# A mixer kernel with TensorE split in two lanes: twelve narrow products instead of four ahead of the next chunk's u, and two seeds at other places

## Chip, cores and metric

One core of a Trainium2 chip. The metric is the device time of one execution in microseconds (us); the median of three runs is given, and one further execution was profiled.

## What is computed

The first step is a short causal convolution with weights that depend on the position (softmax over 7 taps, 8 heads of 24 channels); the second is a mixer over tokens and then over channels. Cut to what matters:

```python
w = softmax(weight_gen)                       # 8 x 4096 x 8 heads x 7 taps
x = sum over k of w[..., k] * x_pad[s + k]    # 8 x 4096 x 192
h = relu(x.T @ w_tok1) @ w_tok2               # over the 4096 tokens, 256 wide
u = x + h.T
out = u + relu(u @ w_ch1) @ w_ch2             # over the channels, 192 -> 1536 -> 192
```

All matrix products are made in more than one pass with operands split into a high part and a low part (`u_hi`, `u_lo`, `w_hi`, `w_lo`), since one pass is not exact enough.

## The kernel before, in words

The 8 x 4096 rows are cut into 64 chunks of 512 rows, `g` = 0 to 63, eight to a sequence. For each chunk TensorE (PE) does four things: six pairs of channel-1 products `ph(p)` (p = 0 to 5, 192 to 1536 channels, written to PSUM tiles `w`), the channel-2 products (into two PSUM banks `acc`: `acc[0]`, the wide part of the sum with three passes, and `acc[1]`, the narrow part with two), the second token product of the next chunk (tile `up`, from which `u` of chunk g + 1 is made), and one first token product (tile `th`) for a chunk of the next sequence. ScalarE (ACT) and VectorE (DVE) turn each `ph(p)` into `h` (`take`: ACT line 799 then DVE line 800 for p < 4; two halves each of lines 792 and 793 for p = 4 and 5), make the taps of the convolution (DVE lines 278 and 292), the parts of u, and the stores (ACT line 897).

The order of all instructions is written out beforehand by a planner in the kernel. It keeps a clock for each engine (`at`, `lane_at`), adds a fixed cost for each operation (`SLOT` 226.7 ns for a 512-column product, `HOP` 60 ns from one engine to another) and issues in the order of these clocks. The engines then run their lists in order, held up by semaphores alone. The planner's costs set the order, not the time on the chip.

In chunks 16 to 54 (`in_lanes`) PE is used as two halves: every product over 128 rows is made as two products over 64 rows, one on the upper half and one on the lower, which run side by side. Each half is a lane with a list of its own (`lanes`); `run_lanes` always issues the product that can start earliest, so PE has one queue in which products of the two lanes alternate. Both lanes add into the same PSUM banks, but never in the same stretch: a bank belongs to the lane that came first (`owner`), and after that lane's last product a no-op on DVE or ACT, whichever the planner has freer (`relay`, line 1389), waits for it; the other lane's first product waits for the no-op (`behind`).

After the six `ph(p)` comes the `section` (line 1467). In it each lane has four lists: `a` and `la`, 36 products each into `acc[0]`; `c` and `lc`, 24 each into `acc[1]`; `u` and `lu`, 10 each into `up`; and 16 each into `th`. The upper lane goes a, u, c, th; the lower lane part of lc, lu, the rest of lc, th, la. So each bank is handed over once. Before the first product into `up` ACT must have copied `xb` into it (line 664, the seed of `up`); before the first product into `th` ACT must have copied the sum so far into it (line 609, `seed_one`). The seed of `up` is issued in `begin`, right behind `take(4)`; the seed of `th` is issued by a hook in the list of a lane (`seed_late`), or, where no hook stands, when the lane reaches the product (`open_one`).

The tiles `w` (for `ph`, `up` and `th`) rotate over three PSUM tiles; `ph(3)` reuses the tile of `ph(0)` and waits for its `take`. The store of a chunk begins when the lower lane has finished `la` (`finish`). One chunk in lanes, the first, has two token products (`early` and `late`), since the lead of the token products is one short there: the kernel makes 40 token products in 39 chunks.

Of the kernel before, what the change touches and what calls it, by code (L numbers as in the profile page):

```python
# [22 lines left out]
def mixer_kernel(ctx: ExitStack, tc: tile.TileContext, x, wg, wt1, wt2, wc1, wc2, out):  # L23
# [798 lines left out]
    def lanes_channel2(g, p):  # L822

        h = [ht[g, p][:, j] if (g, p) in ht else spare[(p - HB) * 2 + j] for j in range(2)]
        parts = []
        for n, steps in ((0, ((A_HI, 0), (A_LO, 0), (A_HI, 1))), (1, ((C_HL, 0), (C_HL, 1)))):
            parts.append([[(SLOT, ("acc", n, g), product(acc_t[g][n], w2s[rows, 2 * p + j, d], h[j][rows, l, :],
                                                      stop=p == NP - 1 and j == 1 and i == len(steps) - 1))
                           for j in range(2) for i, (d, l) in enumerate(steps)] for rows in HALVES])
        return parts  # L830
# [90 lines left out]
    HOP = 60  # L921
# [26 lines left out]
    def on(engine, cost, *after):  # L948
        at[engine] = max(at[engine], *after, 0.0) + cost
        return at[engine] + HOP  # L950

    class Chain:
# [4 lines left out]
        def next(self):  # L957
            self.item = next(self.items, None)
# [23 lines left out]
    def add_chain(items, wait=None, key=None):  # L982

        chains.append(Chain(items, max(at["pe"], at["dve"]) + LOAD if wait is None else wait, key))
# [39 lines left out]
    def need(what, *keys):  # L1024
        while not what():
            state["late"] = True
            at["pe"] += 500
            pump(at["pe"] + SLACK, keys)
        state["late"] = False
# [10 lines left out]
    AHEAD = 2  # L1040
    MOVES = 2
    LANE_TIGHT = 600
    HANDOVER = 60
    state = {"token1": NCH - 1, "token2": -1, "vals": 0, "few": 0, "few_t": 0, "late": False, "jobs": deque(),
             "summed": NCH - 1, "turned": FT - 1, "parts": NCH - 1, "kept": FT - 1, "stored": -1, "out": -1,
             "done": NCH - 1, "w1": NCH + 1, "channel1": 0, "rest": 0, "open": 0}
# [209 lines left out]
    late = ctx.enter_context(tc.tile_pool(name="late", bufs=1))  # L1256
# [65 lines left out]
    def token1_ready(soon=100):  # L1322
        return ready and ready[0][0] in w1t and max(ready[0][1], w1_at.get(ready[0][0], 0.0)) <= at["pe"] + soon
# [21 lines left out]
    lanes, lane_at = [deque(), deque()], [0.0, 0.0]  # L1345
    owner, turn, count = {}, {}, {}
# [3 lines left out]
    def behind(ins, of):  # L1350

        tc.add_manual_dep(ins.ins, of.ins.name, SYNC, reason="a bank goes to the other half of the rows")
# [3 lines left out]
    def lane_start(s):  # L1356

        while lanes[s] and lanes[s][0][0] == 0:
            at["pe"] = max(at["pe"], lane_at[s]) if s == 0 else at["pe"]
            lanes[s].popleft()[2]()  # L1360
        if not lanes[s]:
            return None
        bank, t = lanes[s][0][1], lane_at[s]
        if bank in owner and owner[bank] != s:
            if bank not in turn:
                return None
            t = max(t, turn[bank][1] + HANDOVER)
        return t

    def run_lanes(until):  # L1370

        while True:
            starts = [lane_start(s) for s in range(2)]
            if until():
                return
            s = min((t, s) for s, t in enumerate(starts) if t is not None)[1]
            cost, bank, fn = lanes[s].popleft()
            ins = fn()
            lane_at[s] = starts[s] + cost
            if bank is not None:  # L1380
                if owner.setdefault(bank, s) != s:
                    if bank in turn:
                        behind(ins, turn.pop(bank)[0])
                        owner[bank] = s
                else:
                    count[bank] = count.get(bank, 0) + 1
                    if count[bank] == ITEMS[bank[:2]]:
                        by, eng = min((("dve", nc.vector), ("act", nc.scalar)), key=lambda x: at[x[0]])
                        relay = eng.nop(nofuse=True)  # L1389
                        behind(relay, ins)  # L1390
                        turn[bank] = relay, on(by, 60, lane_at[s] + HOP)
            if s == 0:
                at["pe"] = lane_at[0]

    def hook(fn):

        return 0, None, fn

    def chunk_in_lanes(g):
# [32 lines left out]
        def new_one(first):  # L1432
            m, t = ready.popleft()
            lists, state["open"] = [[], []], m
            owner.update({("th", r, m): first for r in range(KR)})
            return {"m": m, "ready": max(t, w1_at.get(m, 0.0)), "lists": lists, "it": token1(m, lists, first)}

        def seed_one(one):
            next(one["it"])
            t = w_at.popleft()  # L1440
            one["at"] = on("act", 900, one["ready"], t, h1s_at[0]) if one["m"] % NCH else max(one["ready"], t)
# [19 lines left out]
        def spread(items, every=3):  # L1461
            for n, item in enumerate(items):
                if n % every == 0:
                    yield hook(quiet)
                yield item

        def section():
            next(box["two"])
            parts = [lanes_channel2(g, p) for p in range(NP)]
            (a, la), (c, lc) = ([[x for part in parts for x in part[n][s]] for s in range(2)] for n in range(2))  # L1470
            u, lu = ([hook(lambda s=s: not_before(s, box["two_at"])), *box["t2"][s]] for s in range(2))
            late = [hook(lambda s=s: open_one("late", s)) for s in range(2)]
            if "early" in box:
                early = [hook(lambda s=s: open_one("early", s)) for s in range(2)]
                upper = [early[0]] + a + u + [hook(end_two)] + c + [late[0]]
                lower = lc[:8] + [early[1], hook(lambda: end_one("early"))] + lu + lc[8:] + la \
                    + [hook(finish), late[1], hook(lambda: end_one("late"))]
            elif box["late"]:
                upper = a + u + [hook(end_two), *c, late[0], hook(lambda: end_one("late"))]
                lower = lc[:4] + lu + lc[4:14] + [hook(lambda: seed_late(1))] + lc[14:] + [late[1]] + la  # L1480
            else:
                upper = a + u + [hook(end_two)] + c
                lower = lc[:4] + lu + lc[4:] + la
            if not twice:
                lower.append(hook(finish))
            box["end"] = lane_at[0] + sum(x[0] for x in upper) + (twice or box["late"]) * T1
            top.extend(spread(upper))
            top.append(hook(lambda: box.update(done=True)))
            low.extend(lower)

        def seed_late(s):
            need(lambda: token1_ready(20 * SLOT), ("w1", state["token1"] + 1), ("x", state["token1"] + 1))
            one = box["late"] = new_one(s)
            seed_one(one)

        def open_one(key, s):
            if box[key] is True:
                seed_late(s)
            one = box[key]
            if not one["lists"][s]:  # L1500
                next(one["it"])
            not_before(s, one["at"])
            lanes[s].extendleft(reversed(one["lists"][s]))

        def end_one(key):
            t = max(lane_at) + HOP
            pump(t + SLACK_M, (), t + SLACK_A)
            m, it = box[key]["m"], box[key]["it"]
            state["token1"] = m
            free["xh"] = t  # L1510
            next(it, None)
            h1s_at[0] = on("act", 900, t)
            w_at.append(h1s_at[0])
            if m % NCH == NCH - 1:
                h1_at[m // NCH] = on("dve", 1200, on("act", 420, on("dve", 550, w_at[-1])))
            while state["w1"] < min(m + 2, NG - 1):
                state["w1"] += 1
                add_chain(load_w1(state["w1"]), key=("w1", state["w1"]))
# [24 lines left out]
        if not low:  # L1543
            between(at["pe"])
        top.append(hook(lambda: before(0)))
        run_lanes(lambda: "done" in box)

    def not_before(s, t):

        lane_at[s] = max(lane_at[s], t)  # L1550
# [11 lines left out]
    for g in range(NG):  # L1562
# [7 lines left out]
        if lanes[1]:  # L1570
            run_lanes(lambda: not lanes[1])
            at["pe"] = max(at["pe"], lane_at[1])
            need(lambda: g in ut)
# [111 lines left out]
```

## Time and profile before

| | |
|---|---|
| median of three runs | 2068.48 us (2068.37 to 2068.87) |
| the profiled execution's own time | 2068.67 us |
| its span, first to last instruction | 2066.9 us |
| around the span | 1.8 us |
| PE busy with products | 2033.7 us, 98% of the span |
| DVE busy | 1501.7 us, 73% |
| ACT busy | 1449.3 us, 70% |
[...]

Busy time of PE is the time in which at least one product runs. Where two lanes run side by side, a lane that stands still while the other runs does not show in it, and since the ends of products are modelled and overlap, neither does a short gap. What a lane loses is read from the starts of its products in the order of time, and from the list of waits of PE's weight loads (PEld), one of which stands ahead of each product.

### The profile page before, as it was taken

How to read it: one execution, taken by the hardware profiler on the slowest of the kernel's cores; microseconds unless marked ns; L12 is line 12 of the kernel's file. 1: busy time of each engine (PE TensorE's matmuls, PEld its weight loads, DVE VectorE, ACT ScalarE, POOL GpSimd, SP SyncE). 2: the span in 40 equal slices, each digit the busy share in tenths (PEclk: the TensorE clock that was granted, in tenths of full speed). 3: DMA queues.
4: the chain of work that ended last, by engine and by line, in shares of the span. 5: the costliest groups of instructions: out<-in, count | busy, mean ns of one | idle time of the engine just before them, and what ended most of it. 6: DMA issues, size and time to landing. Idle time of an engine off the chain costs nothing.

```text
span 2066.9 us, 39312 instructions
## 1 busy us (share of the span) xinstructions
PE 2033.7 (98%) x16201; PEld 1737.9 (84%) x16201; DVE 1501.7 (73%) x1813; ACT 1449.3 (70%) x2360; POOL 210.6 (10%) x292
## 2 busy tenths in 40 slices
PE   7999999999999999999999999999999999999999
PEld 7878888888888888888888888888888889888887
DVE  9899888888987768777778777768778774343343
ACT  7887667677766676776766677667677667676665
POOL 1101111111111101101101110101100110000000
PEclk9999999999999999999999999999999999999999
DMA  9878778787886766766767666666666663222121
GB/s 337 276 228 230 198 210 230 210 237 199 231 220 174 194 173 167 192 180 171 191 160 197 182 169 185 176 174 190 179 172 181 173 160 117 72 68 62 51 64 24
DMA packets 180928, 361.93 MB, mean 175 GB/s; under 512 B 26138, under 2 KB 129178, under 8 KB 165004
## 3 DMA queue, kind: packets, MB, share of 16 engines
q1 hardware_dynamic: 145420, 225.35, 35.4%
q0 software_dynamic: 35328, 134.07, 27.8%
q8 instruction: 127, 2.08, 0.4%
q14 instruction: 53, 0.43, 0.1%
HBM read 222.77 MB, written 70.52 MB: 142 GB/s over the span
## 4 chain that ended last, share of the span: by engine, by line
PE 79%; DVE 14%; ACT 5%; issue 2%; ACTq 0%; DMA 0%; DVEq 0%
PE acc L469 22%; PE w L469 21%; PE acc L811 15%; PE ph L782 10%; DVE h L800 5%; PE w L782 5%; DVE pr L278 2%; PE up L676 2%; ACT h L799 2%; ACT w L664 2%; PE th L648 2%; DVE pr L292 1%; DVE prk L404 1%; DVE h_spare L793 1%; PE w L676 1%
## 5 line engine op out<-in xcount | busy, mean ns | idle before, releaser
L469 PE MATMUL acc<-h,w2s 64*128 64x512 f32 x3120 | 556.5, 388 | 0.0
L469 PEld LDWEIGHTS acc<-h,w2s 64*128 64x128 f32 x3120 | 441.3, 184 | 34.6
L469 PE MATMUL w<-u_hi,w_hi 64*128 64x512 f32 x1404 | 370.9, 389 | 0.0
L469 PE MATMUL w<-u_hi,w_lo 64*128 64x512 f32 x1404 | 368.7, 387 | 0.0
L469 PE MATMUL w<-u_lo,w_hi 64*128 64x512 f32 x1404 | 368.4, 386 | 0.0
L469 PE MATMUL acc<-h_spare,w2s 64*128 64x512 f32 x1560 | 335.6, 386 | 0.0
L811 PE MATMUL acc<-h,w2s 128*128 128x512 f32 x1400 | 325.6, 390 | 0.0
L799 ACT ACTIVATE h<-w 128x1024 fp32r<-128x1024 f32 x210 | 215.6, 1027 | 148.7 <-PE w L469 80.8
L278 DVE TENSOR_TENSOR pr<-xc,wg 128x768 f32<-128x768 f32 x336 | 313.0, 945 | 0.2
L811 PEld LDWEIGHTS acc<-h,w2s 128*128 128x128 f32 x1400 | 261.8, 188 | 54.4 <-issue 0.7
L800 DVE SCALAR_TENSOR_TENSOR h<-w,h 128x1024 fp32r<-128x1024 f32 x210 | 255.7, 1218 | 71.0 <-ACT h L799 70.5
L296 POOL DMA_DIRECT2D xa<-pr x168 | 146.7, 873 | 1374.2 <-DVE pr L292 1002.2
L469 PEld LDWEIGHTS acc<-h_spare,w2s 64*128 64x128 f32 x1560 | 258.4, 184 | 23.4
L469 PEld LDWEIGHTS w<-u_hi,w_hi 64*128 64x128 f32 x1404 | 250.8, 184 | 24.1 <-DVE h L800 2.9
L469 PEld LDWEIGHTS w<-u_hi,w_lo 64*128 64x128 f32 x1404 | 253.8, 184 | 20.0
L469 PEld LDWEIGHTS w<-u_lo,w_hi 64*128 64x128 f32 x1404 | 254.9, 184 | 17.0
L688 DVE TENSOR_TENSOR uf<-w,uf 64x512 f32<-64x512 f32 x47 | 32.1, 683 | 256.5 <-ACT uf L684 256.5
L897 ACT COPY out_tile<-oa 32x256 f32<-32x256 f32 x504 | 203.7, 404 | 7.6
L469 PE MATMUL w<-w,h 64*128 64x512 f32 x780 | 194.9, 393 | 11.0 <-ACT w L664 11.0
L469 PEld LDWEIGHTS w<-xh,w 64*128 64x128 f32 x1280 | 187.6, 186 | 6.6 <-ACTq L1389 0.8
L469 PE MATMUL w<-xh,w 64*128 64x384 f32 (+1 forms) x1280 | 192.2, 300 | 0.6 <-ACTq L1389 0.4
L469 PEld LDWEIGHTS w<-w,h 64*128 64x128 f32 x780 | 140.7, 184 | 40.3 <-ACT w L664 26.9
(147 smaller groups left out, 3192.3 us busy)
## 6 DMA issues: line engine op xcount, KB each, us to landing
w<-s SPq DMA_DIRECT2D x96, 1024.0 KB, 6.5
xa<-pr POOLq DMA_DIRECT2D x168, 384.0 KB, 4.9
xc<-in_x_dram POOLq DMA_DIRECT2D x42, 960.0 KB, 9.6
out_dram<-out_tile SPq DMA_DIRECT2D x128, 192.0 KB, 2.6
xb<-xs SPq DMA_DIRECT2D x348, 64.0 KB, 5.1
xs<-t SPq DMA_DIRECT2D x56, 384.0 KB, 3.3
raw<-in_moe_w_tok_dram SPq DMA_DIRECT2D x16, 1024.0 KB, 8.3
xc<-in_x_dram POOLq DMA_DIRECT2D x12, 840.0 KB, 10.5
```

Of the source, the lines that this page charges most:

```text
L278: nc.vector.tensor_mul(t.rearrange("p t (h g) -> p (t h) g", h=H).rearrange("p (o n) g -> p o n g", o=1), x_k, w)
L296: nc.gpsimd.dma_start(xat[m].rearrange("p t d -> p (t d)"), tap_sums[m].rearrange("p t d -> p (t d)"), accum_op=ALU.add)
L469: return lambda: nc.tensor.matmul(to, w, v, start=start, stop=stop, skip_group_check=True)
L648: nc.tensor.matmul(to, w[:, c, r * P:(r + 1) * P], xat[m][:, c, :], start=c == first, stop=c == last, skip_group_check=True)
L664: nc.scalar.copy(up.rearrange("p k (n b c) -> p (k n) c b", c=W, b=Q), xb.rearrange("p k (n c b) -> p (k n) c b", c=W, b=Q))
L676: nc.tensor.matmul(up[:, n, :], h1[:, k, d], w[:, l, k * N:(k + 1) * N], start=k == 0 and j == 0 and not seeded, stop=k == KR - 1 and j == ...
L688: nc.vector.tensor_add(u[c, 1, :], up[c, 1, :], u[c, 1, :])
L782: nc.tensor.matmul(ph[:, j, :], w[rows, k, p * P:(p + 1) * P], u[rows, k], start=n == 0, stop=n == len(steps) - 1)
L799: nc.scalar.activation(h[:, :, 0, :], ph, AF.Relu)
L800: nc.vector.scalar_tensor_tensor(h[:, :, 1, :], ph, 0.0, h[:, :, 0, :].bitcast(F32), op0=ALU.max, op1=ALU.subtract)
L811: nc.tensor.matmul(acc[n], w2s[:, f, d], h[:, j, l, :], start=False, stop=f == NF - 1 and i == len(steps) - 1, skip_group_check=True)
L897: nc.scalar.copy(dst, src[to:to + Q].rearrange("p (n e d) -> p n e d", n=2, d=Q)[:, n])
```

## The change

The lower lane's list begins with twelve products into `acc[1]` instead of four ahead of its `up` products (in the chunk with two token products twelve instead of eight, ahead of the early token product). The hook that seeds `th` goes from ahead of lc[14] to ahead of lc[16]; in the chunk with two token products the late `th`, which was seeded when the upper lane reached it, is seeded after twelve products of `c`. The planner's allowance for a handover is 200 ns from the last product to the no-op, counted on the engine of the no-op too, instead of 60 ns behind it.

```diff
-    HANDOVER = 60
+    HANDOVER = 200
...
-            t = max(t, turn[bank][1] + HANDOVER)
+            t = max(t, turn[bank][1])
...
-                        turn[bank] = relay, on(by, 60, lane_at[s] + HOP)
+                        turn[bank] = relay, on(by, 60, lane_at[s] + HANDOVER)
...
             if "early" in box:
                 early = [hook(lambda s=s: open_one("early", s)) for s in range(2)]
-                upper = [early[0]] + a + u + [hook(end_two)] + c + [late[0]]
-                lower = lc[:8] + [early[1], hook(lambda: end_one("early"))] + lu + lc[8:] + la \
+                upper = [early[0]] + a + u + [hook(end_two)] + c[:12] + [hook(lambda: seed_late(0))] + c[12:] + [late[0]]
+                lower = lc[:12] + [early[1], hook(lambda: end_one("early"))] + lu + lc[12:] + la \
                     + [hook(finish), late[1], hook(lambda: end_one("late"))]
             elif box["late"]:
                 upper = a + u + [hook(end_two), *c, late[0], hook(lambda: end_one("late"))]
-                lower = lc[:4] + lu + lc[4:14] + [hook(lambda: seed_late(1))] + lc[14:] + [late[1]] + la
+                lower = lc[:12] + lu + lc[12:16] + [hook(lambda: seed_late(1))] + lc[16:] + [late[1]] + la
             else:
                 upper = a + u + [hook(end_two)] + c
-                lower = lc[:4] + lu + lc[4:] + la
+                lower = lc[:12] + lu + lc[12:] + la
```

## Rows read from the trace of the kernel before

**Rows 1.** The page: busy time of the engines; chain that ended last.

```profile
PE 2033.7 (98%) x16201; PEld 1737.9 (84%) x16201; DVE 1501.7 (73%) x1813; ACT 1449.3 (70%) x2360; POOL 210.6 (10%) x292
...
PE 79%; DVE 14%; ACT 5%; issue 2%; ACTq 0%; DMA 0%; DVEq 0%
```

**Rows 2.** ACT's end copies of token products, 621 to 1712 us: first and last start.

```profile
L637 ACT COPY h1s<-w x35: 786/801/805, 623.0 to 1681.4; 128x768 f32<-128x768 f32 x35
L609 ACT COPY w<-h1s x31: 804/804/805, 640.8 to 1701.6; 128x768 f32<-128x768 f32 x31
```

**Rows 3.** Waits of PE's weight loads, all chunks in lanes: releaser, us, times, longest.

```profile
PEld w L469 <- ACT w L664: 26.9, 38, 0.9
PEld w L469 <- DVE h L800: 2.9, 16, 0.2
PEld w L469 <- ACTq L1389: 0.8, 1, 0.8
PEld w L469 <- ACT w L609: 0.6, 1, 0.6
```

**Rows 4.** Weight loads by time, chunk 25: start us, length, what, [idle before <-releaser].

```profile
883.95 1.09 PEld L469 LDWEIGHTS acc<-h,w2s 64*128 64x128 f32 x9
885.86 0.18 PEld L469 LDWEIGHTS w<-w,h 64*128 64x128 f32 x1 [0.82 <-ACT w L664]
...
885.97 0.19 PEld L469 LDWEIGHTS w<-w,h 64*128 64x128 f32 x1
...
886.21 0.18 PEld L469 LDWEIGHTS w<-w,h 64*128 64x128 f32 x1
```

**Rows 5.** ACT in order of time, same section.

```profile
884.79 1.02 ACT L664 COPY w<-xb 128x1024 f32<-128x1024 f32 x1
...
887.09 0.60 ACT L792 ACTIVATE h_spare<-w 128x512 fp32r<-128x512 f32 x1 [0.76 <-DVE h_spare L793]
887.71 0.82 ACT L897 COPY out_tile<-oa 32x256 f32<-32x256 f32 x2
888.56 0.82 ACT L897 COPY out_tile<-oc 32x256 f32<-32x256 f32 x2
889.39 1.66 ACT L897 COPY out_tile<-oa 32x256 f32<-32x256 f32 x4
891.07 0.80 ACT L609 COPY w<-h1s 128x768 f32<-128x768 f32 x1
```

**Rows 6.** Weight loads in order of time, first token product of chunk 25.

```profile
892.62 0.18 PEld L469 LDWEIGHTS w<-xh,w 64*128 64x128 f32 x1
```

**Rows 7.** Products of PE in order of time, start of `ph(3)` in chunk 26.

```profile
908.04 0.39 PE L469 MATMUL w<-u_hi,w_lo 64*128 64x512 f32 x1
908.19 0.49 PE L469 MATMUL w<-u_hi,w_hi 64*128 64x512 f32 x1
908.27 0.42 PE L469 MATMUL w<-u_hi,w_lo 64*128 64x512 f32 x1
908.52 0.39 PE L469 MATMUL w<-u_hi,w_hi 64*128 64x512 f32 x1
```

**Rows 8.** DVE in order of time, the same stretch of chunk 26.

```profile
906.92 1.21 DVE L800 SCALAR_TENSOR_TENSOR h<-w,h 128x1024 fp32r<-128x1024 f32 x1
```

**Rows 9.** Two stretches of chunk 16: length, busy (x count) of PE, PEld, DVE, ACT, POOL.

```profile
612.00:614.40 2.40, 2.40 (x24) 2.40 (x23) 1.55 (x3) 2.24 (x5) 0.00 (x0) 1.00 1.09 246
616.20:618.60 2.40, 2.32 (x15) 1.64 (x11) 2.04 (x4) 2.27 (x4) 0.00 (x0) 1.00 1.02 313
```

**Rows 10.** ACT in order of time, end of chunk 16.

```profile
615.37 0.61 ACT L726 CAST u_hi<-uf 64x512 fp32r<-64x512 f32 x1
...
617.89 0.79 ACT L609 COPY w<-h1s 128x768 f32<-128x768 f32 x1
```

**Rows 11.** The no-ops that hand banks over, by engine's queue, all chunks in lanes.

```profile
L1389 DVEq EVENT_SEMAPHORE  x174: 21/21/21, 606.4 to 1798.2; - x174
L1389 ACTq EVENT_SEMAPHORE  x62: 17/17/17, 601.8 to 1795.6; - x62
```

## The prediction

> **What bounds the kernel now.** I read the page first, then the waits of TensorE's weight loads, then three engines in order of time in one chunk. The page alone misleads: PE is busy 98% of the span [rows 1], as if nothing were left. But with two lanes a stall of one lane, or a short one of both, hardly shows in busy time. The pace shows it. The copies that end the token products lie 34 intervals apart from 623.0 to 1681.4 us, 31.13 us per chunk [rows 2]. A lane's list for a chunk costs 54 + 36 + 10 + 24 = 124 products of 0.227 us and 16 token products that the planner counts at 0.170 and 0.108 us: 30.34 us. So about 0.8 us per chunk is lost, though PE is "busy".
>
> The waits say where: weight loads waited 26.9 us in 38 of the 39 chunks for the ACT copy of line 664, the seed of `up` [rows 3]. Everything else there is small: 2.9 us for `take(0)` (DVE line 800) in 16 chunks, 0.8 and 0.6 us once each. One such wait in close-up: the run of loads for the narrow sum ends at 885.04, and the load of the first `up` product starts at 885.86, just behind the copy, which ran from 884.79 to 885.81 [rows 4, 5]. PE's products wait in one queue, so the upper lane stands too.
>
> **The change part by part.**
>
> *Twelve products ahead of u.* Nothing is added: the same products, no new instruction or DMA, and eight of `lc` move ahead of `lu`. In chunk 25 the lower lane reaches `up` 8 x 0.227 = 1.81 us later. Its first `up` product now comes about 0.6 us behind its place, so the seed is in time by 1.2 us. What is saved is the wait: 26.9 us less the idle time that lies between loads anyway (pace 0.23 less length 0.18 [rows 4], some 0.04 us each, 1.5 us): **25.4 us**. Its bounds: 26.9 at most, and at least 38 x 0.6 = 23 if only the product's own lateness is lost.
>
> In those rows the load itself waited, the next of its lane came 0.11 us later and the one after that 0.24 us later again [rows 4]. [...]
>
> *What the twelve delay.* The lower lane hands `up` over after 22 products, not 14. The upper lane, which leads by about six (see `ph(3)` below), needs it after 36: 36 - 22 - 6 = 8 products, 1.8 us, are left. The no-op takes 0.02 us [rows 11], and one DVE tap of 0.95 us ahead of it still fits. The rest of `lc` ends at product 34 as before, so `acc[1]`, `th` and `acc[0]` change hands when they did. Cost nothing; without that cover, what the no-op is late by.
>
> *The seed of `th`.* It matters more. ACT does eight copies of line 897 from 887.71 and then this seed, 891.07 to 891.87, without a pause [rows 5]. The token product's load starts at 892.62 [rows 6], so before there was 0.75 us to spare. With the 0.72 us gone the load is due at 891.90: 0.03 us to spare. The hook two products later adds no ACT work ahead of it that I can name, since all eight copies are there already. A handover no-op on ACT would add 0.02 us. I take **0**. Above it: one more pair of copies is 0.82 us [rows 5], less the spare; such a loss would hit the 31 chunks with this seed [rows 2].
>
> *`ph(3)` in every second chunk.* In 16 chunks the first product of `ph(3)` waits for `take(0)`, whose DVE operation ends at 908.13 [rows 3, 8]. The upper lane's product starts at 908.19 and its next at 908.52, 0.33 apart, while the lower lane goes on 908.04, 908.27 [rows 7]. With 2.9/16 less 0.04 for the wait and 0.10 for the slow restart it is 0.24 us. Until now this cost nothing: the lane held back here was held less at `up`, where both waited. With that wait gone it is paid, unless the upper lane may simply trail. Here the new allowance matters. In the chunk with two token products the lower lane's start is set by the upper lane's first eight token products, 4 x (170 + 108) = 1112 ns, plus the handover. Before: 60 + 60 + 60 + 60, in all 1352 ns, just under six products (1360); a lower product was issued just ahead of the upper one six further on and escaped. Now: 200 + 60 + 60, in all 1432 ns, just over; it is issued behind it and is held as well. So I charge it in full: 16 x 0.24 = **3.9 us**. The bounds are 0 and 3.9.
>
> *The chunk with two token products.* Around 616.2 to 618.6 only 15 products start where 24 do in an equal stretch before [rows 9]: the upper lane misses nine, 2.0 us, waiting for the seed of `th`, which ACT makes last, at 617.89 [rows 10]. Issued twelve products of `c` earlier it falls behind the last u_hi copy (done at 615.98) and ends at 616.8; the lane is there at about 616.7. Saved: **1.9 us**. The three u_lo copies behind it move 0.8 us, to 618.8, and are needed only at the seventh product of the next chunk, about 620.3. The early handover (0.8 us once [rows 3]) stays: ACT reaches that no-op when it did. Bounds 0 and 2.7.
>
> *The allowance itself* runs nothing on the chip; it moves the planner's clocks by 0.08 to 0.14 us per handover and may turn the order of an operation. I take 0.
>
> **Sum.** 2068.67 (the profiled execution's own time) - 25.4 - 1.9 + 3.9 = 2045.3. That execution stands 0.2 us above the median, so **2045 us**. A change of 0.2% is 4.1 us.
>
> **The rivals.**
>
> *A, all of it.* The upper lane trails once and `ph(3)` costs nothing: 2068.5 - 25.4 - 1.9 = 2041. For it: the lower lane did escape in [rows 7]. Against: the 1432 ns above.
>
> *B, the wait moves in part to the seed of `th`.* Spare time is 0.03 us, and any no-op or softmax piece ahead of it shows. 0.1 to 0.4 us in 31 chunks: 2045 + 3 to 12, so 2048 to 2057.
>
> *C, no change.* DVE's pieces for `h` are 14% of the chain that ended last [rows 1]. If the ring of three `w` tiles, with `take` as slow as in [rows 8], held `ph(3)`, `ph(4)` and `ph(5)` by 0.24 us each in every chunk, 19 x 0.72 + 16 x 0.48 = 21 us would come back: 2067. Against it: in 19 of these chunks no such wait shows, and DVE has over a quarter of its time free.
>
> *D, slower.* A handover no-op of `up` stands on ACT ahead of the eight copies. It waits for the last of ten `up` products, now at about 889.5, where the copies began at 887.71: everything behind it, the seed of `th` too, is 1.8 us late, and 31 chunks lose it: 2045 + 56 = 2101. It decides from about 0.75 us per chunk on (23.4/31). Against it: the copies are issued in one go behind `take(5)`, and most no-ops, 174 of 236, go to DVE [rows 11].
>
> [...]
>
> **Chances.** The forecast 0.42 (own range 2043 to 2048), A 0.25, B 0.22, C 0.05, D 0.06. Faster by over 0.2%: the forecast, A and B, 0.89. Same: C, 0.05. Slower: D, 0.06. The range 2039.5 to 2057 holds the first three with the bounds of their costs (at its lower end 26.9 and 2.7 saved and nothing paid) and leaves out C and D.
>
> **What would show it.** In the changed kernel's waits of weight loads the line for line 664 should be gone or nearly, and the copies of line 637 should be about 30.5 us apart. The 16 waits for `take(0)` should be there still, with the next lower product now held too; if both lanes run through, it is A. A line for ACT line 609 with some 30 entries is B, and the idle time beside it its price. C would show as waits for line 800 in all chunks; D as waits for line 609 of over 1 us, with ACT idle at line 1389 ahead of line 897. Chunk 16 should be about 2 us shorter. What would make the forecast wrong is above all an order of ACT or DVE turned by the planner's new clocks, which no row of the kernel before can show.

## The result, and the profile after

The changed kernel takes 2046.17 us (median of four runs, 2045.84 to 2046.41), beside 2068.43 us for the kernel before on the same chip (2068.24 to 2068.87): a ratio of 0.9892, 95% interval 0.9875 to 0.9909. Forecast were 2045.0 us within 2039.5 to 2057. The profiled execution took 2046.41 us with a span of 2044.6 us. Both profiled executions had a granted clock of 1.000 and stand 0.24 us above their medians, so they can be compared directly: 22.26 us are gone.

The page of the changed kernel, busy times and the chain that ended last, against [rows 1]:

```profile
PE 2022.3 (99%) x16201; PEld 1741.6 (85%) x16201; DVE 1502.3 (73%) x1813; ACT 1449.5 (71%) x2360; POOL 210.7 (10%) x292
...
PE 95%; DVE 3%; ACT 1%; issue 0%; DMA 0%; ACTq 0%; DVEq 0%
```

The work of every engine is what it was, to 0.1% for DVE and ACT. PE's busy time fell by 11.4 us, half of what the kernel gained; the other half does not show in it. The chain says more: DVE, which stood in it with 14%, is down to 3%.

Waits of PE's weight loads, all chunks in lanes (releaser, us, times, longest), against [rows 3]:

```profile
PEld w L469 <- DVE h L800: 7.5, 18, 0.6
PEld w L469 <- ACTq L1389: 0.8, 1, 0.8
```

The line for the seed of `up` (ACT line 664, 26.9 us in 38 chunks) is gone altogether, the single wait for the seed of `th` (line 609) too. What grew is the wait at `ph(3)` for `take(0)`: 18 times and 7.5 us instead of 16 times and 2.9 us. The list holds only idle times of over about 0.15 us in which neither lane loads, so a shorter wait, or one beside a load of the other lane, is not in it.

The pace, read as in [rows 2] from the end copies of the token products:

```profile
L637 ACT COPY h1s<-w x36: 787/801/805, 621.7 to 1691.0; 128x768 f32<-128x768 f32 x36
```

35 intervals in 1069.3 us are 30.55 us per chunk, where before they were 31.13. From here on I also use the length of single chunks, from the start of the first channel-1 product of a chunk to that of the next. Means over chunks 20 to 51 are 31.20 us (even) and 31.15 (odd) before, 30.74 and 30.46 after. Before, the chunks were alike; now the even ones, where `ph(3)` waits, are 0.28 us longer. The next view shows such a wait, products of PE by time in chunk 26, against [rows 7] ("x2" is two products that the view joins):

```profile
901.11 0.39 PE L469 MATMUL w<-u_lo,w_hi 64*128 64x512 f32 x1
901.16 0.87 PE L469 MATMUL w<-u_hi,w_hi 64*128 64x512 f32 x2
901.53 0.50 PE L469 MATMUL w<-u_hi,w_lo 64*128 64x512 f32 x1
901.87 0.39 PE L469 MATMUL w<-u_hi,w_hi 64*128 64x512 f32 x1
901.87 0.39 PE L469 MATMUL w<-u_hi,w_lo 64*128 64x512 f32 x1
```

Between 901.16 and 901.53 no product starts, at 901.53 one of each lane does (the second of the two joined at 901.16 starts there), and then neither lane starts one until 901.87: the upper lane held by `take(0)` holds the lower one as well. In [rows 7] the lower lane went on.

Why it is every second chunk, DVE and ACT show. In chunk 26 ACT's part of `take(0)` is done at 899.89, but a softmax reduction (line 240) stands ahead of the DVE part, behind the store's pieces, which begin when the lower lane has finished the old chunk (line 887):

```profile
896.82 0.72 DVE L887 STREAM_TRANSPOSE oa<-acc 128x512 f32<-128x512 f32 x1 [0.57 <-PE acc L469]
...
899.73 0.62 DVE L240 TENSOR_REDUCE mx<-wg 128x64 f32<-128x448 f32 x1
900.26 1.21 DVE L800 SCALAR_TENSOR_TENSOR h<-w,h 128x1024 fp32r<-128x1024 f32 x1
```

```profile
898.86 1.03 ACT L799 ACTIVATE h<-w 128x1024 fp32r<-128x1024 f32 x1 [1.38 <-PE w L469]
```

In chunk 27 no such reduction stands there, and DVE waits for ACT:

```profile
930.68 1.22 DVE L800 SCALAR_TENSOR_TENSOR h<-w,h 128x1024 fp32r<-128x1024 f32 x1 [0.24 <-ACT h L799]
```

Counted from the start of the chunk (895.19 and 925.96), `take(0)` ends at 6.28 us in chunk 26 and at 5.94 in chunk 27. The reduction stands there in the even chunks from 18 to 48 alone, and these are 16 of the 18 listed waits; the other two are in chunk 17. No run moved it.

Three more places that the prediction named. The seed of `up` and the seed of `th` on ACT in chunk 25 (against [rows 5]), then the weight loads that needed them (against [rows 4, 6]):

```profile
878.83 1.02 ACT L664 COPY w<-xb 128x1024 f32<-128x1024 f32 x1
...
881.75 0.82 ACT L897 COPY out_tile<-oa 32x256 f32<-32x256 f32 x2
...
885.10 0.80 ACT L609 COPY w<-h1s 128x768 f32<-128x768 f32 x1
```

```profile
880.93 0.18 PEld L469 LDWEIGHTS w<-w,h 64*128 64x128 f32 x1
...
885.96 0.18 PEld L469 LDWEIGHTS w<-xh,w 64*128 64x128 f32 x1
```

The first load for `up` starts 1.08 us after its seed has ended at 879.85. The first load for the token product starts 0.06 us after its seed has ended at 885.90, and no wait is listed for it. But 0.06 us is also the distance at which loads that did wait start behind what they waited for (908.13 and 908.19 in [rows 7, 8]), so a wait too short for the list is not excluded.

The same two stretches of chunk 16 as in [rows 9], and ACT at its end, against [rows 10]:

```profile
612.00:614.40 2.40, 2.40 (x24) 2.27 (x22) 1.60 (x3) 2.24 (x5) 0.00 (x0) 1.00 1.12 255
616.20:618.60 2.40, 2.40 (x28) 2.38 (x25) 2.40 (x4) 2.20 (x4) 0.00 (x0) 1.00 1.04 319
```

```profile
615.33 0.61 ACT L726 CAST u_hi<-uf 64x512 fp32r<-64x512 f32 x1
615.85 0.79 ACT L609 COPY w<-h1s 128x768 f32<-128x768 f32 x1
```

The hole is closed (28 products where 15 started), since the seed now starts right behind the last u_hi copy, at 615.85 and not at 617.89. Chunk 16 lasts 33.47 us instead of 35.57.

### The profile page after: what moved, and what is told of

It reads as the page before. It is cut to its first block, busy times and chain, and to the rows that moved or that the text cites. A ratio compares the mean times of both kernels' runs of the same rounds, so it can differ in the third digit from the quotient of the medians.

```text
span 2044.6 us, 39312 instructions
## 1 busy us (share of the span) xinstructions
PE 2022.3 (99%) x16201; PEld 1741.6 (85%) x16201; DVE 1502.3 (73%) x1813; ACT 1449.5 (71%) x2360; POOL 210.7 (10%) x292
## 4 chain that ended last, share of the span: by engine, by line
PE 95%; DVE 3%; ACT 1%; issue 0%; DMA 0%; ACTq 0%; DVEq 0%
PE w L469 30%; PE acc L469 27%; PE acc L811 15%; PE ph L782 10%; PE w L782 5%; PE up L676 2%; PE th L648 2%; DVE prk L404 1%; PE w L676 1%; PE th L627 1%; PE up L811 1%; PE tapsum L414 1%; DVE h L800 0%; PE acc L848 0%; PE th L629 0%; DVE val L202 0%
## 5 line engine op out<-in xcount | busy, mean ns | idle before, releaser
L469 PE MATMUL acc<-h,w2s 64*128 64x512 f32 x3120 | 517.2, 387 | 0.0
L469 PEld LDWEIGHTS acc<-h,w2s 64*128 64x128 f32 x3120 | 420.7, 184 | 37.1
L469 PE MATMUL w<-u_hi,w_hi 64*128 64x512 f32 x1404 | 361.7, 390 | 0.1
L469 PE MATMUL w<-u_hi,w_lo 64*128 64x512 f32 x1404 | 357.5, 389 | 0.0
L469 PE MATMUL w<-u_lo,w_hi 64*128 64x512 f32 x1404 | 355.0, 387 | 0.0
L469 PE MATMUL w<-w,h 64*128 64x512 f32 x780 | 189.3, 386 | 0.0
L792 ACT ACTIVATE h_spare<-w 128x512 fp32r<-128x512 f32 x156 | 93.4, 599 | 113.3 <-DVE h_spare L793 74.0
```

Source lines behind the costliest of these rows:

```text
L469: return lambda: nc.tensor.matmul(to, w, v, start=start, stop=stop, skip_group_check=True)
L792: nc.scalar.activation(h[:, 0, :], ph[:, j, :], AF.Relu)
```

## The experiments

Three questions were open. What is each part of the change worth alone? What turned the order in which the lanes' products alternate at `ph(3)`? And is that order the whole price of those waits? "Lag" below is how far the lower lane's 21st channel-1 product starts behind the upper lane's, read from the products of PE in chunk 25 (at the planner's 0.227 us a product, beside 0.23 from 908.04 to 908.27 in [rows 7], five products are 1.13 us and six 1.36). The times of the kernel before in the same sessions lay at 2068.2 to 2068.7 us.

| kernel | us | lag | even / odd chunk | waits for line 800 |
|---|---|---|---|---|
| before | 2068.4 | 1.36 | 31.20 / 31.15 | 2.9 us |
| changed | 2046.2 | 1.36 | 30.74 / 30.46 | 7.5 us |
| e1 twelve only | 2041.9 | 1.13 | 30.47 / 30.39 | 3.0 us |
| e2 e1, order turned | 2047.4 | 1.40 | 30.71 / 30.45 | 6.4 us |
| e3 changed, order turned back | 2040.9 | 1.22 | 30.51 / 30.39 | 4.0 us |
| e4 two-token seed only | 2071.7 | 1.53 | 31.44 / 31.17 | 7.3 us |
| e5 lists without allowance | 2045.7 | 1.36 | 30.72 / 30.43 | 7.3 us |
| e6 allowance only | 2072.9 | 1.53 | 31.43 / 31.17 | 6.6 us |
| e8 all 24 first | 2040.4 | 0.90 | 30.43 / 30.42 | 0.8 us |
| e9 smaller lag | 2040.7 | 1.11 | 30.47 / 30.39 | 3.9 us |
| e11 lag under five | 2039.7 | 1.01 | 30.43 / 30.40 | 0.8 us |

**e1: the twelve products alone**, on the kernel before, without the allowance and without the seeds of the two-token chunk:

```diff
-                lower = lc[:4] + lu + lc[4:14] + [hook(lambda: seed_late(1))] + lc[14:] + [late[1]] + la
+                lower = lc[:12] + lu + lc[12:16] + [hook(lambda: seed_late(1))] + lc[16:] + [late[1]] + la
...
-                lower = lc[:4] + lu + lc[4:] + la
+                lower = lc[:12] + lu + lc[12:] + la
```

> Twelve products ahead of u in the 38 chunks with one token product or none; the chunk with two token products and the handover allowance as before. Theory (the forecast's): the wait for the seed of up goes (25.4 us), the seed of th in chunk 16 stays late, and since the lower product is still issued just ahead of its upper partner (1352 ns of lag), the wait at ph(3) in every second chunk costs nothing: 2068.4 - 25.4 = 2043. Rival: the ph(3) wait is paid whatever the order, 16 x 0.24 us: 2047.

2041.9 us (2041.74 to 2042.08), ratio 0.987 (0.9856 to 0.9885). Waits of weight loads, in the same chunks:

```profile
PEld w L469 <- DVE h L800: 3.0, 16, 0.2
PEld w L469 <- ACTq L1389: 0.8, 1, 0.8
PEld w L469 <- ACT w L609: 0.6, 1, 0.6
```

The seed's line is gone here too, but the 16 waits at `ph(3)` stay as short as before, and the part beats the whole by 4.3 us. Moving the products is worth 26.8 us, nearly all of the 26.9 us of waits.

**e2 and e3: the order of the pairs alone.** One line moves a lane's clock in the planner once, by less than a fifth of a product, so that afterwards a lower product is issued behind the upper one and not ahead of it (e2, on e1), or the other way round (e3, on the changed kernel). No product, copy or handover is added, and in the traces the orders of DVE, ACT and GpSimd (POOL) in e2 are those of e1, in e3 those of the changed kernel.

```diff
+        if g == 20:
+            lane_at[1] += 30     # e2, on e1
...
+        if g == 20:
+            lane_at[0] += 40     # e3, on the changed kernel
```

> As twelve only, and from chunk 20 on the planner's clock of the lower lane is set 30 ns later once, so that in each pair the upper product is issued ahead of the lower one; nothing else is changed. Theory: the 15 even chunks from 20 to 48 now pay 0.24 us each at ph(3), both lanes held: 3.6 us more than twelve only. Rival (the order does not matter): the same time as twelve only.

> The changed kernel, and from chunk 20 on the planner's clock of the upper lane is set 40 ns later once, so that in each pair the lower product is issued ahead again. Theory: the 15 even chunks from 20 to 48 no longer pay 0.24 us each: 2046.2 - 3.6 = 2042.6. Rival (the order does not matter): 2046.2.

e2 took 2047.43 us (2047.20 to 2047.63), e3 2040.94 us (2040.82 to 2041.27). Turning the order cost 5.5 us in the one kernel; turning it back won 5.2 us in the other. The waits of e2 first, of e3 below:

```profile
PEld w L469 <- DVE h L800: 6.4, 16, 0.4
```

```profile
PEld w L469 <- DVE h L800: 4.0, 18, 0.6
```

So the order of the two lanes' products in PE's queue is the cause of this price, shown both ways. The lag moves with it, 1.13 to 1.40 us and 1.36 to 1.22. In e1 the upper lane alone is held at `ph(3)` of chunk 18, the lag falls there from 1.43 us at the first channel-1 product to 1.12 at the last, and from then on a held load costs 0.08 us a chunk. In the turned order both lanes are held, the lag stays, and every second chunk pays again. No run has the turned order with a small lag.

It was expected at 3.6 us. The even chunks cost what was expected (0.24 us each between e1 and e2); in the odd chunks, where no wait is listed, another 0.06 us goes. There the same wait is too short for the list. In chunk 27 of the changed kernel `take(0)` ends at 931.90, and the next loads of both lanes start at 931.96, some 0.3 us behind the ones before, where the pace is 0.23 (the line at 931.67 joins two loads, the second starts at 931.96):

```profile
931.66 0.18 PEld L469 LDWEIGHTS w<-u_lo,w_hi 64*128 64x128 f32 x1
931.67 0.47 PEld L469 LDWEIGHTS w<-u_hi,w_hi 64*128 64x128 f32 x2
931.96 0.18 PEld L469 LDWEIGHTS w<-u_hi,w_lo 64*128 64x128 f32 x1
```

In the same chunk of e1 `take(0)` ends at 931.57, and the load of `ph(3)` starts at 931.78, on pace:

```profile
930.35 1.22 DVE L800 SCALAR_TENSOR_TENSOR h<-w,h 128x1024 fp32r<-128x1024 f32 x1 [0.25 <-ACT h L799]
```

```profile
931.56 0.18 PEld L469 LDWEIGHTS w<-u_lo,w_hi 64*128 64x128 f32 x1
...
931.78 0.18 PEld L469 LDWEIGHTS w<-u_hi,w_hi 64*128 64x128 f32 x1
```

**e4, e5, e6: what turned the order.** The seed of the two-token chunk alone, on the kernel before (e4); all lists of the change, with the handover's allowance as it was (e5); the allowance alone, on the kernel before (e6):

```diff
+                upper = [early[0]] + a + u + [hook(end_two)] + c[:12] + [hook(lambda: seed_late(0))] + c[12:] + [late[0]]
+                lower = lc[:12] + [early[1], hook(lambda: end_one("early"))] + lu + lc[12:] + la \
...
-    HANDOVER = 200
+    HANDOVER = 60
-            t = max(t, turn[bank][1])
+            t = max(t, turn[bank][1] + HANDOVER)
-                        turn[bank] = relay, on(by, 60, lane_at[s] + HANDOVER)
+                        turn[bank] = relay, on(by, 60, lane_at[s] + HOP)
```

The first two lines are e4, the rest is e5 against the changed kernel; e6 is the reverse of the rest, on the kernel before.

> The change in the chunk with two token products alone; four products ahead of u and the handover allowance as before. Theory: the upper lane no longer waits 2 us for the seed of th, and the wait for up stays: 2068.4 - 1.9 = 2066.5. Rival: the seed is late for another reason (its data, or ACT's copies ahead of it), and nothing is saved: 2068.4.

> All lists and seeds of the change, the handover allowance as before (60 ns behind the no-op). Theory now: in chunk 16 the earlier seed of th puts ACT's three u_lo copies behind it, so the planner places the no-op for the lower lane's late th after them, the lag of the lower lane grows past six products by this alone, and the order in the pairs is turned without the allowance: 2046, as the changed kernel. Rival (the forecast's arithmetic: 1352 ns against 1360, the allowance turns the order): the lower product stays ahead, 2041.

> The handover allowance of the change alone, all lists as before. Theory: 1432 ns of lag against six products (1360) turn the order in the pairs, the wait for up stays and the lower lane is held at ph(3) as well, as in the run with the two-token part alone but without its 2 us: 2068.7 + 5 = 2073. Rival (an allowance runs nothing on the chip and changes nothing): 2068.5.

e4 took 2071.69 us (ratio 1.0014, 1.0005 to 1.0024): the expectation missed. Chunk 16 did get shorter (33.54 us), but the order turned as well, and every even chunk became 0.24 us longer, with the wait for the seed of `up` still there:

```profile
PEld w L469 <- ACT w L664: 22.8, 38, 0.7
PEld w L469 <- DVE h L800: 7.3, 18, 0.5
```

e5 took 2045.73 us (2045.54 to 2045.98), as good as the whole change: without the allowance the order is turned too. e6 took 2072.92 us (ratio 1.002, 1.0011 to 1.003): the allowance alone turns it as well.

```profile
PEld w L469 <- ACT w L664: 23.3, 38, 0.7
PEld w L469 <- DVE h L800: 6.6, 16, 0.4
```

Either of two parts is enough, and both make the kernel slower when they stand alone. That the seed does it by putting three u_lo copies behind itself on ACT, so that the planner gives the lower lane's start a later time, is worked out from the planner's code and wasn't tried on its own.

**e7: eight products first instead of twelve** (`lc[:8] + lu + lc[8:16]` on the changed kernel), to see whether twelve is needed:

> The changed kernel with eight products ahead of u in place of twelve in the chunks with one token product. Theory: the seed of up is late by about 0.6 us, so 4 x 0.227 = 0.9 us more than before is enough: 2046, the same as twelve. Rival (the whole 1.8 us are needed, because the upper lane's handover or the copies move with it): between the two, about 2055.

2046.23 us (2045.62 to 2046.97), the same as the change, and no wait for line 664. The seed's lateness of 0.6 us is covered by four more products (0.91 us); the other four buy nothing.

**e8: all of `lc` first**, to take the cover of the handover of `up` away:

```diff
-                lower = lc[:12] + lu + lc[12:16] + [hook(lambda: seed_late(1))] + lc[16:] + [late[1]] + la
+                lower = lc + lu[:3] + [hook(lambda: seed_late(1))] + lu[3:] + [late[1]] + la
```

> The changed kernel with all 24 narrow products ahead of u (the seed of th still issued after 27 products). Theory: up is handed over at product 30 of the lower lane (its wide half), just when the upper lane, six ahead, reaches product 36 and needs it; the lower lane's last product must end and the no-op must pass, 0.3 to 0.5 us in some 36 chunks: 2057 to 2064, with waits of weight loads for line 1389. Rival (handing over costs nothing as long as the lower lane is done in time): 2046.

The theory fell: 2040.44 us in one run, and no such wait. The upper lane lost time once, in chunk 17 (31.72 us long, 31.02 in the changed kernel), why is not shown; the lag came out at 0.90 us, and what vanished is the waits at `ph(3)`:

```profile
PEld w L469 <- DVE h L800: 0.8, 2, 0.6
```

So the cover of that handover can't be judged from e8. What the run suggested is that the lag itself decides.

**e9 and e11: a smaller lag.** The changed kernel, with the upper lane's clock in the planner moved on once in chunk 18, by 420 ns (e9) and by 565 ns (e11):

```diff
+        if g == 18:
+            lane_at[0] += 420    # e9; e11: 565
```

> The changed kernel, and the planner's clock of the upper lane set 420 ns later once, at chunk 18, so that the lower lane lags about 1270 ns behind the upper instead of 1385. Theory: take(0) is then done when the upper lane reaches ph(3), no chunk waits there any more (as in the run with all 24 products first), and 36 chunks take 30.41 us each where the changed kernel took 1101.6 us for them: 2046.2 - 6.4 = 2039.8. Rival (only the order in the pairs counts, not the size of the lag): 2041, as with the order turned back.

> The changed kernel with the upper lane's clock in the planner moved on by 565 ns in chunk 18, so that the planned lag of the lower lane is about 1120 ns, just under five products, where the smaller lag of the run before left about 1270 ns. Theory: what decides at the fourth channel-1 pair is how many products the lower lane really trails on the chip, and a planned order in which the lower product stands ahead of the upper one five further on makes that five instead of six. The upper lane then reaches the pair one product, 0.2 us, later, the evacuation is in time, no waits for DVE line 800 are left, all chunks last about 30.41 us, and the time is about 2040.0 us. Rival: the smaller planned lag does nothing more than the turned order did; waits for line 800 in every second chunk stay, even chunks last 30.47 and odd ones 30.39, and the time stays at 2040.7 us. Third: the handover of the second token product's tile, with one product less of cover, shows as waits for no-ops of line 1389; 0.1 us in 38 chunks would make it 2044.

e9 took 2040.67 us (2040.39 to 2040.93) and kept its waits, so its theory fell and its rival held. e11 took 2039.72 us (2039.67 to 2039.81), ratio 0.9862 (0.9845 to 0.9878); it lost them, as its theory said, and is the fastest kernel here, faster than both given ones. Weight loads by time at `ph(3)` of chunk 26, e9 first, e11 below:

```profile
900.09 0.18 PEld L469 LDWEIGHTS w<-u_hi,w_hi 64*128 64x128 f32 x1 [0.19 <-DVE h L800]
900.09 0.18 PEld L469 LDWEIGHTS w<-u_hi,w_lo 64*128 64x128 f32 x1
900.20 0.19 PEld L469 LDWEIGHTS w<-u_hi,w_hi 64*128 64x128 f32 x1
900.20 0.19 PEld L469 LDWEIGHTS w<-u_hi,w_lo 64*128 64x128 f32 x1
900.43 0.18 PEld L469 LDWEIGHTS w<-u_lo,w_hi 64*128 64x128 f32 x1
```

```profile
899.85 0.18 PEld L469 LDWEIGHTS w<-u_hi,w_lo 64*128 64x128 f32 x1
899.99 0.18 PEld L469 LDWEIGHTS w<-u_hi,w_hi 64*128 64x128 f32 x1
900.07 0.18 PEld L469 LDWEIGHTS w<-u_hi,w_lo 64*128 64x128 f32 x1
900.16 0.19 PEld L469 LDWEIGHTS w<-u_hi,w_hi 64*128 64x128 f32 x1
```

DVE's `take(0)`, e9 first, e11 below:

```profile
898.82 1.21 DVE L800 SCALAR_TENSOR_TENSOR h<-w,h 128x1024 fp32r<-128x1024 f32 x1
```

```profile
898.72 1.22 DVE L800 SCALAR_TENSOR_TENSOR h<-w,h 128x1024 fp32r<-128x1024 f32 x1
```

In e9 `take(0)` ends at 900.03 and the load follows at 900.09. In e11 it ends at 899.94 and the load follows at 899.99; it too may have waited for it, but beside a load of the other lane, and its product starts at 900.16, 0.23 us behind the one before, on time. The chunk itself starts at 894.01 and 894.00. At that moment the lower lane has four products of the old chunk still to start in e11, in e9 five. So it finishes the old chunk 0.10 us sooner against the upper lane (lag 1.11 and 1.01): the store's first piece on DVE (line 887) starts at 895.28 and not at 895.38, and `take(0)`, which stands behind it and line 240 in DVE's queue, comes 0.10 us sooner. ACT's part is done 0.34 and 0.37 us before that. In e9 the held load cost the chunk 0.08 us, since it comes in time for its product but the next loads then follow late.

**e10: the seed of `th` made twice**, which puts one more copy of 0.80 us on ACT ahead of the token product and leaves the values as they are:

```diff
             nc.scalar.copy(th[:, :, cols], h1s[b])
+            if lists is not None and m > NCH * 3 + 1:
+                nc.scalar.copy(th[:, :, cols], h1s[b])
```

> The changed kernel with the ACT copy that seeds th made twice, into the same tile, in the chunks from 17 on: 0.8 us more on ACT ahead of the token products. Theory (the forecast's): the seed has no time to spare in the changed kernel, so nearly all of it is lost in 31 chunks, 0.7 to 0.8 us each: 2068 to 2071, with some 31 waits of weight loads for line 609. Rival: ACT has time there (it stands idle for 1.8 us behind the seed), and the copy is hidden: 2046 to 2050.

2070.78 us (2070.29 to 2071.16), 24.6 us more than the changed kernel. The lines of the kernel move by two, so 611 is the second copy:

```profile
PEld w L469 <- ACT w L611: 23.6, 33, 0.8
PEld w L469 <- DVE h L802: 7.5, 18, 0.6
```

24.6 us over 33 waits are 0.75 us of the 0.80: the time to spare is about 0.05 us.

## Why the prediction was right, step by step

*The wait for the seed of `up`: right.* 25.4 us were expected, with 26.9 as the upper bound; e1 measures 26.8. The deduction of 0.04 us per wait for the idle time between loads was too careful. A likely reason, not tried, is that the held load also slowed the loads behind it [rows 4]. The lead that the seed has now, expected at 1.2 us, is 1.08 in chunk 25.

*`ph(3)` is paid once the other wait is gone, and in full: right, and mis-sized.* Both lanes stand, as the rows at 901.53 and 901.87 show. 3.9 us were expected and 5.2 to 5.5 measured (e3, e2). The 0.24 us per even chunk was the right price for these (0.24); of the rest about 0.9 us is the 0.06 us of the odd chunks, which the sum did not have: there `take(0)` is late too, but by less.

*Why the order turns: half right.* The step that failed is the sentence that puts it down to the allowance, 1352 ns against 1432. The allowance does turn the order (e6), but so does the two-token seed alone (e4, e5), which was counted as a pure gain. Taking the allowance back would have saved next to nothing (e5, 2045.7 us). Had only the two-token part been made, the forecast would have had the wrong sign: 1.9 us less expected, 3.0 us more measured.

*Chunk 16: the right place, too large a net gain.* Expected were 1.9 us; the chunk itself gave 2.1. Chunk 17 gives some back, since `ph(3)` waits there as well:

```profile
PEld w L469 <- DVE h L800: 0.9, 2, 0.6
```

These are the changed kernel's waits of weight loads from 612 to 652 us; e1 has no wait for line 800 there. Between e1 and e9, whose later chunks are alike, chunk 16 gains 1.98 us, chunks 17 and 18 lose 0.67 (31.00 and 30.91 us where e1 has 30.52 and 30.72), and 1.3 us are left. The copies of u_lo were in time, as expected: the last ends at 618.45, and the first product with u_lo starts at 620.4. What the sum put at nothing is a late `take(0)` in chunk 17: ACT's part of it starts at 623.16, 4.11 us behind the chunk's start, and in e1 at 624.92, 3.79 behind it. The lower lane's first product comes only 0.05 us later than in e1 (1.54 and 1.49 us behind the upper lane's), so its start alone doesn't explain this; why the copy is late is open.

*The seed of `th` has no time to spare but is in time: right.* 0.03 us were expected, 0.06 us stand between the rows at 885.90 and 885.96, and e10 gives 0.05. The 0.72 us that the expectation took off is nowhere worked out; 25.4 us over 38 chunks would be 0.67 and leave 0.08. Rival B, a wait in its place, was real in mechanism and price, and stayed out by that little.

*The handovers cost nothing: right.* Line 1389 holds one load for 0.8 us, as before. That 1.8 us of cover is what keeps it so was not shown, since e8 changed the lag too.

*The rivals.* A, 2041 us, is what e3 and e9 are: the whole gain, with the order unturned (e1 too, without the two-token part). C and D did not occur: in the odd chunks from 19 on no wait for line 800 is listed, and in chunk 25 the copies of line 897 follow the last half of `take(5)` without a no-op of a handover ahead of them.

The measured sum is then 2068.7 - 26.8 + 5.3 - 1.3 = 2045.9, with 2046.2 measured. The forecast came within 1.2 us because three terms were off in directions that partly cancel: 1.4 us too little for `up`, 1.4 too little for `ph(3)`, 0.6 too much for chunk 16. That they cancel is luck. So is, in part, that `ph(3)` was charged in full: the two-token part would have turned the order without the 1432 ns. A slip without effect is the lower end of the range: 26.9 and 2.7 us off 2068.7 are 2039.1, not 2039.5.

## What to carry to other kernels

Where two streams share one queue in order, a stall can have two prices: here an even chunk lasted 0.08 us longer than an odd one with the held product issued behind its partner (e1), and 0.26 us longer with it issued ahead (e2); read from the trace who else stands still before charging it. Wherever an order is planned ahead, a change of a cost or of a copy's place can turn that order for the rest of the run, so look at the order that the changed plan issues, and run each part alone: here one part was worth 26.8 us, and two others cost 3 and 4 us by themselves. If a wait is 0.2 us at the end of a chain that another lane starts, starting that lane a little sooner may remove most of its price for nothing; here 0.10 us sooner did. And look at what stands in the queue ahead of the late piece: here a reduction of 0.62 us stood there in every second chunk, and moving it was not tried.

## What the runs showed of the hardware

In chunk 26 of e9 the upper lane's weight load waits for `take(0)`, with 0.19 us in which neither lane loads, and the load of the other 64 rows, for which no wait is listed, starts at 900.09 with it and not sooner. A load that passes another load's wait does not occur in these rows of e9.

That held load has its cost although its own product comes in time, at 900.16, 0.22 us behind the one before: the upper lane's next loads start at 900.20 and 900.43, 0.11 and 0.23 us apart, and an even chunk of e9 lasts 0.08 us longer than an odd one.

Busy time of PE was 99% both at 2046.2 us and at 2039.7 us, and of weight loads 85% and 92%, as the page of the fastest kernel (e11) shows, though it issues the same 16201 loads:

```profile
PE 2016.1 (99%) x16201; PEld 1865.1 (92%) x16201; DVE 1501.6 (74%) x1813; ACT 1449.3 (71%) x2360; POOL 210.3 (10%) x292
```

Yet e9 stands at 86% with 2040.7 us and e10 at 87% with 2070.8. Counted one by one, 16201 loads of 0.18 us [rows 4] would be 2916 us, over the 1865.1 us of busy time and over the whole span: the busy time counts loads that overlap once. So that share follows how far the loads of the two lanes overlap, and here it told little of the time.
